# Where a 64-bit weight piece is finished, and how the queues around it are ordered, in a top-k attention kernel with an MLP behind it

## The chip, the cores and the metric

The kernel runs on one core of a Trainium2 chip. Its engines are TensorE (matrix multiply, PE in the profile; its weight loads are PEld), VectorE (DVE), ScalarE (ACT), GpSimd (POOL) and SyncE (SP), which issues the transfers. The metric is the device time of one execution in microseconds (us); less is better.

## The reference

Attention over 8 batches, 8 heads, 576 positions and a head width of 64, in which each query keeps only its 32 largest scores; the result, 4608 tokens of 512 numbers, goes through an MLP with 2048 hidden units and a SmeLU between its two matrix products. `moe_w_in` and `moe_w_out` come as 64-bit floats; q, k and v have 32 bits.

```python
scores = scale * np.matmul(q, k.transpose(0, 1, 3, 2))
kth = np.partition(scores, -top_k, axis=-1)[..., -top_k:-top_k + 1]
scores = np.where(scores >= kth, scores, -1000000000.0)
attn = np.exp(scores - np.max(scores, axis=-1, keepdims=True))
attn = attn / (np.sum(attn, axis=-1, keepdims=True) + 1e-09)
x = np.matmul(attn, v)                     # then (B,H,S,D) -> (B*S, H*D)
h = x @ w_in
g = np.where(h >= 1, h, np.where(h <= -1, 0.0, (h + 1) ** 2 / 4.0))
out = (g @ w_out).astype(np.float32)
```

## The kernel before

**Steps.** Attention is done in 144 steps, in the order of the list `steps`. A step takes 128 queries of two heads of a batch (or the 64 tail queries of four heads). `queries` and `keys_of` transpose q and k on TensorE; `scores` (L211) multiplies them in two halves of 288 columns and ScalarE copies the result into the tile `s` (three buffers). `weights` (L236) does the top-k on VectorE: `pairs` (L231) takes the larger of column c and column c + 288, four rounds of `max` (eight largest values, L248) and `match_replace` (L257) find the 32 largest of these pairs, and L262 to L269 repair the 32nd value `kth` with the smaller ones of the pairs. After the first round the row maxima are negated (`nmax`, L250, on POOL) and ScalarE takes the exponentials `e` (L252). L279 zeroes what lies below `kth` and sums up; L284 and L285 give the reciprocal `rz`, and POOL normalises `e` with it (L287). `transpose_w` (L291) turns the weights on TensorE, `values` (L305) multiplies them by v and ScalarE copies the result into `xT`.

**Can the pairs go wrong?** Where more large values sit in pairs than the repair looks at, `excess` (L270, on POOL) is positive. At the end `judge` reduces all of `excess` to a flag, and if it is set, `run` is done once more by a general path (`paired` false) without pairs. For the inputs used here the flag is not set.

**The MLP.** When all steps of a chunk (one or two tiles of 128 tokens) are done, `mlp` (L337) puts its work into `pending`: 16 units `hidden` (matmuls into `ph`, L344, then two relus on ScalarE, L348 and L350, and three POOL operations, L351 to L353; `r` has two buffers, `ph` three), then per tile eight units `final` (L361). A unit has a cost and the number of weight pieces that it needs.

**Weights.** The 64-bit weights are brought to 32 bits on the chip in 64 pieces of 128 x 256 (`weight_piece`, L80): a load of both words (`raw`, three buffers); VectorE shifts the high word (L87), ScalarE makes units of the low word (L90) and the absolute value (L94), POOL adds as integers (L91); one piece later VectorE puts the sign bit in (L96) and multiplies by "is at least 1.125 * 2^-15" (L98; the high word read as a 32-bit float, in which this bound stands for the smallest normal 32-bit number), which makes tiny weights zero.

**Order.** PE, DVE and ACT run in the order in which the program is written (`manual_schedule`, L425); POOL's and SP's order is left to the scheduler of the language. The loop of L466 writes it: iteration m does `values` of step m - 2, `scores` of step m + 1 and `weights` of step m, cut into seven slots; slot 2 has `transpose_w` of step m - 1, slot 4 transposes of later queries and keys, each slot but some first ones converts a piece, and `advance` (L413) takes units from `pending` by a share of what is left and by estimates of when each engine is where (`pe_time`, `dve_time`, `K_TIME`, `PIECE_TIME`).

## Time and profile before

| | |
|---|---|
| time, median of 3 runs | 1894.29 us (1892.67 to 1895.69) |
| profiled execution | 1893.17 us, its span 1891.4 us |
| mean granted TensorE clock | 0.947 of full speed |
| busy share of the span | PE 89%, PEld 62%, DVE 82%, ACT 53%, POOL 53% |
| moved by DMA | 57.81 MB |

The span runs from the first to the last instruction of the profiled execution; the time of an execution has a little around it. A busy share is a mean over stretches with different limits, so it tells little alone. A row of a timeline has the start, the duration, the engine, the line and operation, the tile written and those read, and in brackets how long the engine stood idle before it and what released it. A row of waits says who waited for whom, how long in total, how often, and the longest.

### The profile page before, as it was taken

The numbers are of one execution on the slowest core, as the hardware profiler recorded it, in microseconds if no ns is written. First come the engines' busy times: TensorE is split into PE (matmuls) and PEld (weight loads), VectorE is DVE, ScalarE is ACT, GpSimd is POOL, SyncE is SP. The second block draws the span as 40 slices with busy tenths as digits, with TensorE's granted clock in tenths as the row PEclk, the third lists the DMA queues.
The fourth block names the chain that finished last, engine by engine and source line by source line (L and its number), as shares of the span: only waits on it lengthen the run. The fifth ranks groups of instructions, "written<-read, shape, count | busy, mean of one in ns | idle before, by whom it ended". The sixth has DMA issues, their size and how long they took to land.

```text
span 1891.4 us, 33291 instructions
## 1 busy us (share of the span) xinstructions
PE 1688.7 (89%) x10513; PEld 1178.2 (62%) x10513; DVE 1558.9 (82%) x4947; ACT 1004.1 (53%) x2525; POOL 996.3 (53%) x1853
## 2 busy tenths in 40 slices
PE   3464599989999999999999999989999999998998
PEld 2252366666677666757576676656576666666665
DVE  5858777888878998999998898999887888869760
ACT  5454455556555654555464665555555555455443
POOL 3463355656556372817282674628283564653653
PEclk7576799999999999999999999999999999999999
DMA  7323100100001100110010100110010000000000
GB/s 188 99 68 92 62 18 18 38 21 24 10 17 39 29 12 23 32 36 13 17 34 25 24 12 25 36 32 12 23 32 18 18 12 10 12 12 6 1 12 14
DMA packets 107450, 57.81 MB, mean 31 GB/s; under 512 B 86272, under 2 KB 94464, under 8 KB 107264
## 3 DMA queue, kind: packets, MB, share of 16 engines
q1 hardware_dynamic: 107264, 55.59, 10.7%
q8 instruction: 85, 1.39, 0.3%
q14 instruction: 101, 0.83, 0.1%
HBM read 46.14 MB, written 9.44 MB: 29 GB/s over the span
## 4 chain that ended last, share of the span: by engine, by line
PE 60%; DVE 17%; POOL 12%; ACT 5%; issue 5%; DMA 1%; POOLq 0%; SPq 0%; DVEq 0%; ACTq 0%
PE py L361 24%; PE ph L344 15%; PE sp L223 8%; PE po L313 6%; PE pw L298 4%; DVE tops L248 4%; POOL g L353 4%; DVE more L257 4%; POOL r L352 3%; DVE e L279 3%; POOL r L351 2%; POOL e L287 2%; ACT e L252 1%; DVE seconds L265 1%; ACT s L226 1%
## 5 line engine op out<-in xcount | busy, mean ns | idle before, releaser
L344 PE MATMUL ph<-xT,w_in 128*128 128x128 f32 (+1 forms) x3200 | 564.6, 332 | 26.3 <-ACT g L350 23.9
L361 PE MATMUL py<-w_out,g 128*128 128x512 f32 x1152 | 538.4, 607 | 50.3 <-DVE w_out L98 47.6
L344 PEld LDWEIGHTS ph<-xT,w_in 128*128 128x128 f32 x3200 | 484.3, 197 | 100.4 <-ACT g L350 35.7
L248 DVE MAX8 tops<-more 128x8 f32<-128x288 f32 x1152 | 465.6, 446 | 0.0
L361 PEld LDWEIGHTS py<-w_out,g 128*128 128x128 f32 x1152 | 207.3, 192 | 280.8 <-issue 218.0
L257 DVE MATCH_REPLACE8 more<-tops,more 128x288 f32<-128x288 f32 x864 | 375.9, 443 | 0.0
L287 POOL TENSOR_SCALAR e<-e,rz 128x576 f32<-128x576 f32 x288 | 218.1, 767 | 237.8 <-DVE rz L285 215.5
L348 ACT ACTIVATE r<-ph,half 128x128 f32<-128x128 f32 (+1 forms) x400 | 166.9, 417 | 286.3 <-POOL g L353 210.2
L270 POOL TENSOR_TENSOR excess<-seconds,kth 128x2 f32<-128x2 f32 x144 | 60.7, 421 | 403.3 <-DVE kth L269 402.3
L279 DVE SCALAR_TENSOR_TENSOR e<-s,kth,e 128x576 f32<-128x576 f32 x288 | 242.4, 869 | 37.0 <-ACT e L252 36.9
L353 POOL TENSOR_TENSOR g<-r,g 128x128 f32<-128x128 f32 (+1 forms) x400 | 256.8, 642 | 28.5
L223 PE MATMUL sp<-kT,qT 64*128 64x288 f32 x1024 | 199.3, 454 | 53.3 <-ACT xT L326 43.7
L352 POOL TENSOR_TENSOR r<-r 128x128 f32<-128x128 f32 (+1 forms) x400 | 226.7, 567 | 29.9
L252 ACT ACTIVATE e<-s,nmax 128x576 f32<-128x576 f32 x288 | 215.8, 782 | 44.6 <-POOL nmax L250 44.6
L234 DVE TENSOR_TENSOR more<-s 128x576 f32<-128x576 f32 x144 | 115.9, 805 | 145.2 <-ACT s L226 145.1
L226 ACT ACTIVATE s<-sp 128x288 f32<-128x288 f32 x576 | 197.1, 418 | 49.0 <-PE sp L223 44.8
L351 POOL TENSOR_SCALAR r<-r 128x128 f32<-128x128 f32 (+1 forms) x400 | 177.4, 443 | 62.2 <-ACT r L348 61.6
L298 PEld LDWEIGHTS pw<-ident,e 128*128 128x128 f32 x1152 | 136.7, 145 | 76.3 <-issue 38.2
L299 ACT COPY wT<-pw 128x512 f32<-128x512 f32 x288 | 154.8, 595 | 52.1 <-PE pw L298 52.1
L298 PE MATMUL pw<-ident,e 128*128 128x128 f32 x1152 | 157.4, 281 | 26.4 <-POOL e L287 25.0
L313 PEld LDWEIGHTS po<-wT,v_in 128*64 128x64 f32 x2048 | 119.9, 142 | 95.7 <-issue 55.9
L313 PE MATMUL po<-wT,v_in 128*64 128x128 f32 x2048 | 156.8, 290 | 25.2 <-ACT wT L299 24.2
(60 smaller groups left out, 1476.9 us busy)
## 6 DMA issues: line engine op xcount, KB each, us to landing
q_in<-in_q_dram SPq DMA_DIRECT2D x32, 256.0 KB, 3.1
k_in<-in_k_dram SPq DMA_DIRECT2D x64, 128.0 KB, 3.1
raw<-in_moe_w_in_dram SPq DMA_DIRECT2D x32, 256.0 KB, 2.7
v_in<-in_v_dram SPq DMA_DIRECT2D x8, 1024.0 KB, 5.7
raw<-in_moe_w_out_dram SPq DMA_DIRECT2D x32, 256.0 KB, 2.6
out_dram<-y SPq DMA_DIRECT2D x32, 256.0 KB, 2.3
k_tl<-in_k_dram SPq DMA_DIRECT2D x8, 128.0 KB, 3.1
v_tail<-in_v_dram SPq DMA_DIRECT2D x16, 64.0 KB, 2.8
```

What stands on the lines that cost most here:

```text
L223: nc.tensor.matmul(o[:, a0 - c0:a1 - c0], qT[d, g, :], kT[d, g, k0:k0 + a1 - a0], start=True, stop=True)
L248: nc.vector.max(out=tops[:, i, r:r + 8], in_=src[:, i, :])
L252: nc.scalar.activation(e[:, i, :], s[:, i, :], AF.Exp, bias=nmax[:, i:i + 1])
L257: nc.vector.match_replace(out=rest[:, i, :], in_to_replace=tops[:, i, r:r + 8], in_values=src[:, i, :], imm_value=LOWEST)
L279: nc.vector.scalar_tensor_tensor(out=e[:, i, :], in0=s[:, i, :], scalar=last[:, i:i + 1], in1=e[:, i, :], op0=ALU.is_ge, op1=ALU.mult, acc ...
L287: nc.gpsimd.tensor_scalar(e[:, i, :], e[:, i, :], rz[:, i:i + 1], 1.0, ALU.mult, ALU.mult)
L298: nc.tensor.transpose(pt[:, c, :], w[:, i, main(i)][:, c * P:(c + 1) * P], ident)
L313: nc.tensor.matmul(po[j * D:(j + 1) * D], v_in[:, h, c, :] if c < NT else v_tl[0][:, h, :], wT[:, j, c, :] if c < NT else wTt, start=(c == ...
L344: nc.tensor.matmul(ph, w_in[:, kk, f * P:(f + 1) * P], xT[:, kk, 0:cw], start=(kk == 0), stop=(kk == NK - 1))
L352: nc.gpsimd.tensor_tensor(out=r, in0=r, in1=r, op=ALU.mult)
L353: nc.gpsimd.tensor_tensor(out=g[:, 0:cw], in0=r, in1=g[:, 0:cw], op=ALU.add)
L361: nc.tensor.matmul(py, gs[f][:, i * P:(i + 1) * P], w_out[:, f, :], start=(f == 0), stop=(f == NF - 1))
```

## The change

- A piece has one VectorE operation left, the shift. ScalarE takes the sign of the high word instead of its absolute value, and POOL multiplies magnitude and sign into the weight tile.
- Tiny weights are no longer zeroed on the way. After all pieces are converted, `inspect_piece` loads each piece once more, one per step, and ScalarE sums the signs of weight + 1.125 * 2^-15 and of weight - 1.125 * 2^-15; `judge` takes the difference of the sums into `excess`, so that a tiny weight sets the flag, and the general path (`any_size`) zeroes it. No weight of the inputs used here is that small.
- `nmax` and `excess` are made on VectorE instead of POOL.
- Iteration m begins the scores of step m + 2 instead of m + 1 and transposes the queries of step m + 3 instead of m + 2.
- POOL joins the order written by hand. After the conversion the top-k of a step is written into slots 0 to 3 (`parts`), which places its normalisation on POOL in slot 3 instead of slot 6. `advance` and the estimates of time are rewritten: a unit is taken only if its pieces are usable by the estimate, and the share is bounded by what is pending until the next chunk is ready.

```diff
@@ -71,51 +77,52 @@
             nc.gpsimd.memset(x, 0.0)
 
 
+
+    WC = 256
+    n_pieces = NK * DFF // WC + NF * DM // WC
     n_steps = B * (NT * NHP + NHP // 2)
-    excess = const.tile([P, 2 * n_steps], F32, name="excess")
-
-
-    WC = 256
-
-    def weight_piece(pool, dst, src):
+    excess = const.tile([P, 2 * n_steps + n_pieces], F32, name="excess")
+    signs = const.tile([P, 2, n_pieces], F32, name="signs")
+
+
+    pieces_of_weights = [(w_in[:, kk, c:c + WC], moe_w_in[kk * P:(kk + 1) * P, c:c + WC])
+                         for c in range(0, DFF, WC) for kk in range(NK)]
+    pieces_of_weights += [(w_out[:, f, c:c + WC], moe_w_out[f * P:(f + 1) * P, c:c + WC])
+                          for f in range(NF) for c in range(0, DM, WC)]
+
+    def load_words(pool, i):
         raw = pool.tile([P, 2 * WC], U32, name="raw", bufs=3)
-        nc.sync.dma_start(out=raw, in_=src.bitcast(U32))
+        nc.sync.dma_start(out=raw, in_=pieces_of_weights[i][1].bitcast(U32))
         words = raw.rearrange("p (n t) -> p n t", t=2)
-        lo, hi = words[:, :, 0], words[:, :, 1]
+        return words[:, :, 0], words[:, :, 1]
+
+    def convert_piece(pool, i, any_size):
+
+        lo, hi = load_words(pool, i)
+        dst = pieces_of_weights[i][0]
 
         bits = pool.tile([P, WC], U32, name="bits", bufs=2)
         nc.vector.tensor_scalar(bits, hi, 3, None, ALU.logical_shift_left)
 
         units = pool.tile([P, WC], F32, name="units", bufs=2)
         nc.scalar.activation(units, lo, AF.Identity, bias=two, scale=2.0 ** -51)
+        sign = pool.tile([P, WC], F32, name="sign", bufs=2)
+        nc.scalar.activation(sign, hi.bitcast(F32), AF.Sign)
         nc.gpsimd.tensor_tensor(out=bits.bitcast(I32), in0=bits.bitcast(I32), in1=units.bitcast(I32), op=ALU.add)
-
-        size = pool.tile([P, WC], F32, name="size", bufs=2)
-        nc.scalar.activation(size, hi.bitcast(F32), AF.Abs)
-        yield
-        nc.vector.scalar_tensor_tensor(out=bits, in0=hi, scalar=0x80000000, in1=bits,
-                                       op0=ALU.bitwise_and, op1=ALU.bitwise_or)
-        nc.vector.scalar_tensor_tensor(out=dst, in0=size, scalar=1.125 * 2.0 ** -15, in1=bits.bitcast(F32),
-                                       op0=ALU.is_ge, op1=ALU.mult)
-
-    def weight_pieces(pool):
-
-        pieces = [(w_in[:, kk, c:c + WC], moe_w_in[kk * P:(kk + 1) * P, c:c + WC])
-                  for c in range(0, DFF, WC) for kk in range(NK)]
-        pieces += [(w_out[:, f, c:c + WC], moe_w_out[f * P:(f + 1) * P, c:c + WC])
-                   for f in range(NF) for c in range(0, DM, WC)]
-        before = None
-        for dst, src in pieces:
-            piece = weight_piece(pool, dst, src)
-            if before is not None:
-                next(before, None)
-            next(piece)
-            before = piece
-            yield
-        next(before, None)
-        yield
-
-    n_pieces = NK * DFF // WC + NF * DM // WC
+        if any_size:
+            nc.scalar.activation(units, hi.bitcast(F32), AF.Abs)
+            nc.vector.scalar_tensor_tensor(out=sign, in0=units, scalar=TINY, in1=sign, op0=ALU.is_ge, op1=ALU.mult)
+
+            nc.vector.tensor_scalar(bits.bitcast(F32), bits.bitcast(F32), LARGEST, -LARGEST, ALU.min, ALU.max)
+        nc.gpsimd.tensor_tensor(out=dst, in0=sign, in1=bits.bitcast(F32), op=ALU.mult)
+
+    def inspect_piece(pool, i):
+
+        _, hi = load_words(pool, i)
+        for x in range(2):
+            sign = pool.tile([P, WC], F32, name="sign", bufs=2)
+            nc.scalar.activation(sign, hi.bitcast(F32), AF.Sign, bias=tiny[:, x:x + 1],
+                                 accum_out=signs[:, x, i:i + 1])
 
 
     def run(ctx, paired):
@@ -247,7 +254,7 @@
                 for i in range(2):
                     nc.vector.max(out=tops[:, i, r:r + 8], in_=src[:, i, :])
                 if r == 0:
-                    nc.gpsimd.tensor_scalar(nmax, tops[:, :, 0], -1.0, 1.0, ALU.mult, ALU.mult)
+                    nc.vector.tensor_scalar(nmax, tops[:, :, 0], -1.0, None, ALU.mult)
                     for i in range(2):
                         nc.scalar.activation(e[:, i, :], s[:, i, :], AF.Exp, bias=nmax[:, i:i + 1])
                         if i == 0:
@@ -267,7 +274,7 @@
                                         in1=seconds, op=ALU.min)
                 for i in range(2):
                     nc.vector.max(out=kth[:, i, :], in_=tops[:, i, TOP_K - 1:TOP_K + 8])
-                nc.gpsimd.tensor_tensor(out=excess[:, 2 * m:2 * m + 2], in0=seconds[:, :, 7], in1=kth[:, :, 0],
+                nc.vector.tensor_tensor(out=excess[:, 2 * m:2 * m + 2], in0=seconds[:, :, 7], in1=kth[:, :, 0],
                                         op=ALU.subtract)
                 last = kth[:, :, 0]
             else:
@@ -395,34 +402,43 @@
         ready = [max(m for m in range(n) if steps[m][3] == ch) for ch in range(len(chunks))]
 
         mlp_pool = ctx.enter_context(tc.tile_pool(name="mlp", bufs=1))
-        pieces_left = weight_pieces(mlp_pool) if paired else None
         pending = deque()
         total, spent = sum(len(tiles) for tiles in chunks) * (NK * NF + NF * DM // P), 0
-        converted, due = (-1 if paired else n_pieces), 0.0
+        converted, inspected, due = 0, 0, 0.0
 
         def convert():
             nonlocal converted
             if converted < n_pieces:
+                convert_piece(mlp_pool, converted, not paired)
                 converted += 1
-                next(pieces_left)
-
-
-        K_TIME, PIECE_TIME, UNIT_TIME, SLOTS = 9.6, 1.2, 0.22, 7
-        pe_time, dve_time, done, scored = 9.0, 12.0, {}, {}
+
+        def inspect():
+            nonlocal inspected
+            if paired and inspected < n_pieces:
+                inspect_piece(mlp_pool, inspected)
+                inspected += 1
+
+
+        K_TIME, PIECE_TIME, UNIT_TIME, SLOTS = 9.8, 0.4, 0.22, 7
+        pe_time, dve_time, done, scored, usable = 9.0, 12.0, {}, {}, {}
 
         def advance(amount, until=0.0):
 
             nonlocal spent, due, pe_time
             due += amount
-            while pending and pending[0][1] <= converted and (due >= pending[0][0] or pe_time < until):
-                cost, _, work = pending.popleft()
+            while pending and (due >= pending[0][0] or pe_time < until):
+                cost, pieces, work = pending[0]
+                if pieces > converted or usable[pieces] > pe_time + 0.5:
+                    break
+                pending.popleft()
                 due = max(due - cost, 0.0)
                 spent += cost
                 pe_time += cost * UNIT_TIME
                 work()
-            due = min(due, 8.0)
-
-        order = tc.manual_schedule(engines={mybir.EngineType.PE, mybir.EngineType.DVE, mybir.EngineType.Activation})
+            due = min(due, 16.0)
+
+        order = tc.manual_schedule(engines={mybir.EngineType.PE, mybir.EngineType.DVE, mybir.EngineType.Activation,
+                                            mybir.EngineType.Pool})
         order.__enter__()
         keys, xTs = {}, {}
         q_ins, qTs = {}, {}
@@ -452,51 +468,66 @@
             state.append(dict(m=m, t=t, hp=hp, keys=keys[b], qT=qTs[b, t], xT=(xTs[ch], col)))
             scores(state[m])
 
-        queries(0)
-        begin(0)
-        scored[0] = pe_time
+        def begin_at(m):
+            nonlocal pe_time
+            if m < n:
+                queries(m)
+                begin(m)
+                pe_time += 1.15
+                scored[m] = pe_time + 2.0
+
+        def convert_by(time):
+            convert()
+            usable[converted] = time
+
+        begin_at(0)
         if paired:
-            convert()
-            convert()
             pairs(state[0])
-        for _ in first:
-            pass
+        convert_by(13.0)
+        convert_by(14.0)
+        next(first)
+        begin_at(1)
         fetch(1)
         next_keys = 1
         for m in range(n + 2):
-            share = (total - spent) / (n + 2 - m)
+            coming = min((r + 2 - m for r in ready if r + 2 > m), default=1)
             if 2 <= m:
+                pe_time = max(pe_time, transposed + 1.8) + 1.25
                 values(state[m - 2])
                 state[m - 2] = None
-                pe_time += 1.25
                 for ch in [c for c in range(len(chunks)) if ready[c] == m - 2]:
                     pending.extend(mlp(xTs[ch], chunks[ch], mlp_pool))
-            if m + 1 < n:
-                begin(m + 1)
-                pe_time += 1.15
-                scored[m + 1] = pe_time + 2.0
-            top_k, quota = None, 0
+            share = min((total - spent) / (n + 2 - m), sum(work[0] for work in pending) / coming)
+            if m > 0:
+                begin_at(m + 2)
+            else:
+                for _ in first:
+                    pass
+                begin_at(2)
+            top_k, parts = None, [0] * SLOTS
             if m < n:
                 top_k = weights(state[m], state[m + 1] if m + 1 < n else None)
-                quota = min(SLOTS, n_pieces - converted)
+                left = min(SLOTS, n_pieces - converted)
+                parts = [1] * SLOTS if left > 0 else [1, 2, 2, 2, 0, 0, 0]
                 start = max(dve_time, scored[m])
-                dve_time = start + K_TIME + PIECE_TIME * quota
+                dve_time = start + K_TIME + PIECE_TIME * left
                 done[m] = dve_time
             for slot in range(SLOTS):
-                if top_k is not None:
+                now = start + (dve_time - start) * (slot + 1) / SLOTS
+                for _ in range(parts[slot]):
                     next(top_k, None)
-                    if slot > 0 or m % 2 == 0:
-                        convert()
-                    until = start + (dve_time - start) * slot / SLOTS
-                else:
-                    until = 0.0
+                if m < n and converted < n_pieces:
+                    convert_by(now)
+                elif slot == 6:
+                    inspect()
                 if slot == 2 and 1 <= m <= n:
                     pe_time = max(pe_time, done[m - 1] + 2.0) + 1.0
                     transpose_w(state[m - 1])
+                    transposed = pe_time
                 if slot == 2 and m == n and paired:
                     judge(ps, att)
                 if slot == 4:
-                    queries(m + 2)
+                    queries(m + 3)
                     if m < n and prep is None and next_keys < B and steps[m][0] == next_keys - 1 and steps[m][1] >= 1:
                         prep = keys_of(next_keys)
                     if prep is not None and m % 2 == 0:
@@ -506,7 +537,7 @@
                             prep, next_keys = None, next_keys + 1
                         else:
                             keys[next_keys] = got
-                advance(share / SLOTS, until)
+                advance(share / SLOTS if m < n else 0.0, now)
             for _ in (top_k if top_k is not None else ()):
                 pass
         while pending:
@@ -518,6 +549,7 @@
 
     def judge(ps, att):
         worst = att.tile([P, 8], F32, name="worst", bufs=1)
+        nc.vector.tensor_tensor(out=excess[:, 2 * n_steps:], in0=signs[:, 0], in1=signs[:, 1], op=ALU.subtract)
         nc.vector.max(out=worst, in_=excess)
         pt = ps.tile([1, P], F32, name="pworst", tag="a", bufs=4)
         nc.tensor.transpose(pt, worst[:, 0:1], ident)
```

## Rows read from the trace of the kernel before

**Rows 1.** Windows: stretch; busy us of PE, PEld, DVE, ACT, POOL; clock, DMA.

```profile
0.00:247.00 247.00, 131.73 (x670) 90.28 (x671) 175.93 (x555) 125.92 (x313) 111.30 (x196) 0.70 0.34 97
247.00:1843.00 1596.00, 1515.64 (x9614) 1060.43 (x9613) 1382.14 (x4391) 863.98 (x2171) 865.66 (x1607) 0.98 0.08 21
```

**Rows 2.** Windows of the tile rz on VectorE alone (one per step).

```profile
0.00:247.00 247.00, 1.66 (x10) 0.70 0.34 97
247.00:1843.00 1596.00, 22.18 (x134) 0.98 0.08 21
```

**Rows 3.** Waits, 0 to 247 us: total, times, longest.

```profile
PE py L361 <- DVE w_out L98: 47.6, 13, 6.4
DVE bits L96 <- POOL bits L91: 44.8, 32, 17.4
```

**Rows 4.** Waits, 247 to 1843 us.

```profile
POOL excess L270 <- DVE kth L269: 391.7, 77, 5.9
...
ACT r L348 <- POOL g L353: 188.4, 158, 3.3
DVE more L234 <- ACT s L226: 140.2, 80, 8.0
...
DVE e L279 <- ACT e L252: 36.6, 36, 3.1
```

**Rows 5.** Groups by line: busy us, mean ns, idle before and releaser.

```profile
L270 POOL TENSOR_TENSOR excess<-seconds,kth 128x2 f32<-128x2 f32 x144 | 60.7, 421 | 403.3 <-DVE kth L269 402.3 <-ACT wTt L302 1.1
...
L91 POOL TENSOR_TENSOR bits<-bits,units 128x256 int32<-128x256 int32 x64 | 50.2, 785 | 117.2 <-ACT units L90 48.3 <-DVE bits L87 39.8 <-DVE z L284 23.8
...
L284 DVE TENSOR_SCALAR z<-z 128x2 f32<-128x2 f32 x144 | 39.1, 271 | 4.7
...
L250 POOL TENSOR_SCALAR nmax<-tops 128x2 f32<-128x2 f32 x144 | 28.2, 196 | 0.4 <-DVE tops L248 0.4
...
L96 DVE SCALAR_TENSOR_TENSOR bits<-raw,bits 128x256 uint32<-128x256 uint32 x64 | 26.9, 421 | 44.8 <-POOL bits L91 44.8
...
L98 DVE SCALAR_TENSOR_TENSOR w_out<-size,bits 128x256 f32<-128x256 f32 x32 | 14.9, 467 | 3.4
...
L185 ACT ACT_TABLE_LOAD x1 | 1.3, 1283 | 0.7 <-PEq L547 0.7
```

**Rows 6.** Timeline of the conversion, VectorE and POOL: start us, us.

```profile
15.23 0.82 DVE L248 MAX8 tops<-more 128x8 f32<-128x288 f32 x2
...
74.04 2.02 POOL L287 TENSOR_SCALAR e<-e,rz 128x576 f32<-128x576 f32 x2
...
77.88 0.29 DVE L87 TENSOR_SCALAR bits<-raw 128x256 uint32<-128x256 uint32 x1
78.08 0.81 DVE L248 MAX8 tops<-more 128x8 f32<-128x288 f32 x2
...
78.88 0.73 POOL L91 TENSOR_TENSOR bits<-bits,units 128x256 int32<-128x256 int32 x1 [1.97 <-ACT units L90]
...
115.09 0.29 POOL L351 TENSOR_SCALAR r<-r 128x128 f32<-128x128 f32 x1 [1.15 <-ACT r L348]
...
116.38 0.29 POOL L351 TENSOR_SCALAR r<-r 128x128 f32<-128x128 f32 x1
```

**Rows 7.** Timeline of two steady steps on VectorE: start us, us.

```profile
643.02 0.17 DVE L285 RECIPROCAL rz<-z 128x2 f32<-128x2 f32 x1
...
648.66 0.76 DVE L262 TENSOR_TENSOR more<-s 128x576 f32<-128x576 f32 x1
...
653.20 0.17 DVE L285 RECIPROCAL rz<-z 128x2 f32<-128x2 f32 x1
...
658.84 1.20 DVE L262 TENSOR_TENSOR more<-s 128x576 f32<-128x576 f32 x1
```

**Rows 8.** Windows of line 344 on TensorE alone.

```profile
0.00:247.00 247.00, 31.07 (x224) 0.70 0.34 97
```

**Rows 9.** DMA issues by line: count, KB each, us to landing.

```profile
raw<-in_moe_w_in_dram SPq DMA_DIRECT2D x32, 256.0 KB, 2.7
```

## What the change should do to the time: the prediction

> **What bounds the kernel now.** I read the page's slices first, then busy time by stretches, then the times at which the steps end, then the waits of those stretches, last the timeline of single steps. A step ends on VectorE with the reciprocal `rz` (L285), one per step, 144 in all. The view of that line by windows splits the run [rows 2]: the first 247 us hold 10 of them, the next 1596 us the other 134, of which the first falls right at its border: the work of 11 steps lies before 247 us and that of 133 behind it. 48.4 us of the span remain for what follows the last step (the last tile's MLP). So a step costs 22.5 us in the first stretch and 12.0 us in the second.
>
> In the first stretch [rows 1] the reader is to see that no engine is full: TensorE is busy 132 of 247 us at a granted clock of 0.70 (a mix of its two levels, 1.2 and 2.4 GHz), VectorE 176. VectorE waits 44.8 us for the integer add on POOL in the middle of a piece, and TensorE 47.6 us for converted `w_out` [rows 3]. This stretch is a chain through the weight pieces. In the second stretch TensorE is busy 1516 of 1596 us and VectorE 1382, so two engines are nearly full; VectorE waits 140.2 us for scores and 36.6 us for exponentials [rows 1, 4], and 37 us are short gaps. TensorE has 80 us of idle time in all of it: that caps what any cure of VectorE's waits can bring.
>
> **Conversion, part by part.** Per piece the change takes the and/or (421 ns) and the compare-multiply (about 460 ns) off VectorE and leaves the shift, which holds the queue 0.20 us from start to start (77.88 to 78.08) [rows 5, 6]. Sign on ScalarE takes the place of Abs, one for one; I price it the same. POOL keeps the add and gets a multiply of the same shape and two sources, which before has no row; the add is the nearest, 0.73 us alone, 785 ns mean [rows 5, 6]. It cannot cost less than nothing; above, I bound it by that mean.
>
> A step with seven pieces then is: on VectorE 10.18 us (an undisturbed step, 643.02 to 653.20 [rows 7]) + 7 x 0.20 + 0.40 (negation and difference, below) = 12.0. On POOL: 7 x 2 x 0.73 + 2.0 (normalisation, the 74.04 row [rows 6]) = 12.2. Both now end together, and they disturb each other: the pairwise maximum L262 took 0.76 us with POOL idle and 1.20 us with POOL at work [rows 7]. Four VectorE operations of a step have two long sources (L262, L234, twice L279), so 4 x 0.44 = 1.8 is added: 14.0 us. The bits, units and sign tiles have two buffers, so VectorE's shift also waits for the multiply two pieces back; POOL's in-order queue puts the normalisation between two pieces, and that 2 us is already in POOL's sum. The raw loads land in 2.7 us [rows 9]; with about 1 us of ScalarE behind them and three buffers, that is some 1.2 us a piece, below POOL's 1.46.
>
> Two pieces precede step 0, then seven a step: 62 / 7, so nine steps convert, against 9.8 in the old pattern of six and seven. The first maximum started at 15.2 us behind two pieces [rows 6]; now the pairs come first, say 14. Nine steps at 14.0 reach 140. In the last four of them the first tile's 16 hidden units want POOL at 1.29 us each (115.09 to 116.38 [rows 6]), 20.6 us, which either fit into gaps (0) or lie wholly on POOL's chain: 140 to 161, I take 150. Two steps without pieces at 11.5 follow: the eleventh step ends at 173 (163 to 184) instead of 247. **This is 74 us, the surest part.** TensorE will by then have done a little less MLP than the 28 hidden units (224 records of 8) seen before 247 [rows 8], about 5 us of debt, absorbed below.
>
> *A rule against it:* here the row shows POOL at 0.73 to 0.79 us for what VectorE's multiply did in about 0.46. The Trainium skill, "GPSIMD Engine Reference", section Engine selection, says that elementwise work on a tile belongs on VectorE, POOL being about twice slower with two inputs; the trace agrees on the ratio (1.7). By the rule the multiply stays on VectorE, whose step would be 12.0 + 7 x 0.5 = 15.5 us plus contention, nine steps 14 us or more slower than the sum above: the rule is right on the operation and wrong on the queue.
>
> **The steady stretch.** Maxima are negated on VectorE and `excess` is formed there: two operations of 128x2, 133 times. The nearest rows are operations of 128x2 there: 0.17 us for the reciprocal of an undisturbed step [rows 7], 271 ns mean for L284 [rows 5]; between them I take 0.20, the distance at which a short operation lets the next one start [rows 6]. So 0.40 us a step = 53 us (45 to 72), all on an engine that is nearly full. What it buys: POOL loses 89 us (28.2 + 60.7) and, more, the place where its queue stood 391.7 us for the 33rd value [rows 4, 5] with MLP units behind it; ScalarE, which stood 188.4 us for POOL's last operation of a unit, is released earlier. Scores two steps ahead give the pairs one more step of slack, 12 us, where the longest wait was 8.0: I take three quarters of the 140.2 (105) as gone, the rest standing where TensorE itself is a step behind; and half of the 36.6 (18), since the exponentials no longer pass POOL but still stand behind ScalarE's other work. VectorE's account: 1596 - 105 - 18 + 53 = 1526. TensorE's floor is its 1516 plus the debt. Two bounds so near each other alternate by phase of the MLP, so a quarter of TensorE's 80 idle us stays on top: 1546.
>
> Later inspection: 64 pieces are loaded again, one a step, with two Signs each. At about 430 ns like Abs plus a read of the sum that no row shows (VectorE's own is 80 ns), about 1 us of ScalarE a step. ScalarE is busy 864 of 1596 [rows 1], which hides it; uncovered it would be 64 us. Its loads join SP's queue behind query loads; 16 MB over 700 us, with the DMA share at 0.08, collide with nothing. The slot pattern (two parts of the top-k per slot) moves no work on VectorE's own queue.
>
> **Sum.** 173 + 1546 + 48.4 = 1767 span, plus 1.8 around it (the profiled execution took 1893.17 for a span of 1891.4) = 1769; that execution lies 1.1 below the median of 1894.29. Forecast: **1770**.
>
> **The rivals.**
> - *Only the start gains.* TensorE had 80 us idle in 1596, and VectorE gets 53 us more work: the second stretch may stay at 1596. 163..184 + 1596 + 48 + 2 gives 1809 to 1830. For it: TensorE 95% busy. Against: 177 us of waits. 0.27.
> - *Both waits vanish.* The stretch falls to TensorE's 1516: 163 + 1516 + 50 = 1729, a little lower if busy TensorE hides stretched matmuls. 0.09.
> - *Slower: POOL in program order.* POOL joins the manual schedule, and a step's normalisation is now placed with the fourth slot, ahead of the MLP units of slots 3 to 6, though it waits for that step's `rz`. Those units, and through two `r` buffers ScalarE's relus, stand until VectorE ends the step; the second exponential of the next step stands behind them. VectorE wants it 8 us into its 10.2 us step. After `rz` POOL needs 2 us, then 1.29 a unit or more: (8 - 2 - 0.8) / 1.29 = 4 units fit. 400 hidden units lie in about half of the steps, 5.6 a step, of which 5/7 stand ahead, 4.0; the two `r` buffers take two off. From four units on each further one costs 1.29 us in some 67 steps; 1.4 of them beyond eat all 124 us of the forecast, and two give 1770 + 173 = 1943. Against it: POOL stood as long before, for `excess`. 0.09.
> - *Sign is not in the loaded table.* The trace shows one table load, 1283 ns [rows 5], so all functions used so far sit together; none is Sign. If it sits elsewhere, at most four switches a step with two exponentials in nine steps and two in 64 later ones: 164 x 1.28 = 210 us on ScalarE, between hidden and all on the path; half of it gives 1875, all of it 1980. 0.03. The Trainium skill, "ScalarE: Activation LUTs", section Table sets, lists relu, copy, identity and abs as in every set and does not name Sign there; with the 2.66 us per switch that the page gives for load and drain it would be 436 us.
>
> The forecast's own case has 0.52 (1740 to 1805). What a measurement of this kernel can tell from no change is about 0.2%. The slow sign holds 0.09 and part of the table case, 0.11; within 0.2% 0.02; faster 0.87. The range must reach over the start-only case and to the PE floor: 1715 to 1840, leaving out the slow cases and the extremes.
>
> **What would show it.** Right: the eleventh `rz` near 173; VectorE's waits for POOL's add gone, short waits for the multiply in their place; POOL about 85% busy until 150; waits for scores under 50 us in all; undisturbed steps of 10.6 us. Wrong: the ninth step later than 180 (POOL's queue costs more than its operations); steps of 12 us or more after it, with VectorE waiting for `e` (POOL's order) or TensorE without gaps (start only); more than one table load.

## The result, and the profile after

The changed kernel takes 1831.41 us (median of 4; 1829.49 to 1835.5), the kernel before beside it 1893.48: ratio 0.967 [0.966, 0.969]. That is 62 us less, where 124 were forecast; 1831 lies within the range 1715 to 1840, near its slow end. The profiled execution took 1835.5 us, its span 1833.5. Of all executions below one stands out and is left out of its ratio: one of the four of *h1* took 9250 us instead of 1823, and no trace shows why.

Windows of the changed kernel, cut where the eleventh and the last step end (columns as in [rows 1]):

```profile
0.00:205.30 205.30, 127.75 (x674) 89.85 (x675) 150.95 (x450) 130.31 (x324) 146.41 (x238) 0.75 0.44 125
205.30:1776.70 1571.40, 1507.47 (x9600) 1056.10 (x9599) 1428.88 (x4655) 926.09 (x2418) 788.46 (x1339) 0.98 0.11 31
1776.70:1833.50 56.80, 48.20 (x242) 29.97 (x240) 1.21 (x5) 13.58 (x42) 21.41 (x56) 0.97 0.03 12
```

The start got 42 us shorter (247 to 205; 173 forecast), the second stretch 25 (1596 to 1571; 1546 forecast), the tail got 8 longer (48.4 to 56.8). All three terms came out dearer than forecast: by 32, 25 and 8 us.

Waits of VectorE in the changed kernel, whole run:

```profile
DVE e L286 <- ACT e L259: 46.2, 39, 5.9
DVE bits L105 <- POOL w_out L117: 24.0, 8, 10.5
DVE e L286 <- issue: 22.2, 12, 3.4
DVE e L286 <- POOL g L360: 21.3, 8, 4.6
DVE e L286 <- POOL r L359: 16.2, 8, 4.3
DVE more L241 <- ACT s L233: 12.4, 1, 12.4
```

The reader is to see two things beside [rows 3, 4]. The wait for scores (140.2) is gone from the second stretch; the 12.4 is the first step. But L286, the operation that needs the exponentials, now waits 106 us there (109 in the whole run), under several names, where it waited 36.6. VectorE's account of that stretch is 1429 busy + 106 + 36 short gaps = 1571, against 1382 + 177 + 37 before: of 140 us that left, 70 came back one line further down, and 47 more of work are, in the main, the moved operations.

ScalarE and POOL in the changed kernel, whole run:

```profile
POOL e L294 <- DVE rz L292: 524.6, 80, 15.1
...
ACT r L355 <- POOL g L360: 149.7, 137, 6.4
```

In the kernel before, whole run:

```profile
POOL e L287 <- DVE rz L285: 215.5, 68, 7.9
...
ACT r L348 <- POOL g L353: 210.2, 190, 3.3
```

ScalarE still waits for POOL's last operation of a unit. POOL no longer stands for `excess` (402.3 us before [rows 5]), but stands longer for `rz`.

Groups by line of the changed kernel (busy us, mean ns, idle before and releaser):

```profile
L257 DVE TENSOR_SCALAR nmax<-tops 128x2 f32<-128x2 f32 x144 | 39.5, 275 | 4.9
...
L105 DVE TENSOR_SCALAR bits<-raw 128x256 uint32<-128x256 uint32 x64 | 32.5, 509 | 36.8 <-POOL w_out L117 24.0 <-DMA raw<-in_moe_w_in_dram 6.4 <-POOL w_in L117 5.8
...
L277 DVE TENSOR_TENSOR excess<-seconds,kth 128x2 f32<-128x2 f32 x144 | 30.1, 209 | 5.0
...
L117 POOL TENSOR_TENSOR w_in<-sign,bits 128x256 f32<-128x256 f32 x32 | 25.6, 801 | 2.5
...
L192 ACT ACT_TABLE_LOAD x1 | 1.3, 1283 | 0.7 <-PEq L579 0.7
```

POOL's multiply costs what the add was priced at. The shift, the same operation as before, has a mean of 509 ns. A conversion step of the changed kernel, parts of its timeline, shows why:

```profile
50.05 0.28 DVE L105 TENSOR_SCALAR bits<-raw 128x256 uint32<-128x256 uint32 x1
...
55.00 0.73 POOL L111 TENSOR_TENSOR bits<-bits,units 128x256 int32<-128x256 int32 x1
55.08 0.80 DVE L105 TENSOR_SCALAR bits<-raw 128x256 uint32<-128x256 uint32 x1 [1.29 <-POOL w_in L117]
55.80 0.81 DVE L255 MAX8 tops<-more 128x8 f32<-128x288 f32 x2
...
57.30 0.73 POOL L117 TENSOR_TENSOR w_in<-sign,bits 128x256 f32<-128x256 f32 x1
57.38 0.80 DVE L105 TENSOR_SCALAR bits<-raw 128x256 uint32<-128x256 uint32 x1
...
60.95 0.75 DVE L269 TENSOR_TENSOR more<-s 128x576 f32<-128x576 f32 x1
60.95 1.32 POOL L117 TENSOR_TENSOR w_in<-sign,bits 128x256 f32<-128x256 f32 x1
```

With POOL idle, as at 50.05, the shift takes 0.28; where it begins just behind an add or multiply of POOL it takes 0.80 and ends 0.15 us after that operation. At 60.95 it is POOL's operation that is stretched. They take turns; the 8-largest operations show nothing of it. The Trainium skill, "SBUF — State Buffer", section SBUF: two separate sides, states such a rule: VectorE and GpSimd share a pair of ports as an exclusive lock held for a whole instruction, wanted by VectorE's operations with two inputs or in a fast mode. The trace agrees on the turns, 0.80 us against 0.28; whether the shift, which has one source, works in such a mode no run shows.

In the same kernel, where the MLP begins, VectorE and POOL:

```profile
103.92 0.73 POOL L117 TENSOR_TENSOR w_out<-sign,bits 128x256 f32<-128x256 f32 x1
104.62 0.30 POOL L358 TENSOR_SCALAR r<-r 128x128 f32<-128x128 f32 x1
...
115.84 0.46 POOL L360 TENSOR_TENSOR g<-r,g 128x128 f32<-128x128 f32 x1
116.25 0.72 POOL L111 TENSOR_TENSOR bits<-bits,units 128x256 int32<-128x256 int32 x1
117.05 0.73 POOL L117 TENSOR_TENSOR w_out<-sign,bits 128x256 f32<-128x256 f32 x1
117.82 0.37 DVE L105 TENSOR_SCALAR bits<-raw 128x256 uint32<-128x256 uint32 x1 [10.48 <-POOL w_out L117]
```

Nine hidden units (1.28 us each) run between two pieces, and VectorE's shift waits 10.5 us for a buffer. And a step of the second stretch:

```profile
408.79 0.32 DVE L257 TENSOR_SCALAR nmax<-tops 128x2 f32<-128x2 f32 x1
...
413.67 0.37 ACT L355 ACTIVATE r<-ph,half 128x128 f32<-128x128 f32 x1 [2.11 <-POOL g L360]
...
415.45 0.37 ACT L355 ACTIVATE r<-ph,half 128x128 f32<-128x128 f32 x1 [1.16 <-POOL g L360]
...
419.69 0.77 ACT L259 ACTIVATE e<-s,nmax 128x576 f32<-128x576 f32 x1
420.55 0.82 DVE L286 SCALAR_TENSOR_TENSOR e<-s,kth,e 128x576 f32<-128x576 f32 x1 [3.70 <-POOL g L360]
```

The maxima are there at 409.1, the exponential starts at 419.7: ScalarE works in program order, and between the two it stands in relus that wait for one of two `r` buffers, which POOL empties. Four such waits make up 4.1 of the 10.6 us; the rest is, in the main, work that stands ahead of the exponential.

### The profile page after: what moved, and what is told of

Read it like the earlier page. It is cut to its first block, busy times and chain, and to the rows that moved or that the text cites. A ratio compares the mean times of both kernels' runs of the same rounds, so it can differ in the third digit from the quotient of the medians.

```text
span 1833.5 us, 33329 instructions
## 1 busy us (share of the span) xinstructions
PE 1683.4 (92%) x10513; PEld 1175.9 (64%) x10513; DVE 1581.0 (86%) x5108; ACT 1070.0 (58%) x2781; POOL 956.3 (52%) x1631
## 4 chain that ended last, share of the span: by engine, by line
PE 56%; DVE 26%; POOL 9%; ACT 4%; issue 3%; DMA 1%; POOLq 0%; SPq 0%; ACTq 0%; DVEq 0%
PE py L368 21%; PE ph L351 16%; PE sp L230 7%; DVE tops L255 7%; DVE more L264 6%; PE po L320 5%; PE pw L305 4%; DVE e L286 4%; POOL g L360 3%; POOL r L359 2%; DVE seconds L272 2%; DVE more L269 2%; DVE more L241 2%; POOL e L294 2%; POOL r L358 1%
## 5 line engine op out<-in xcount | busy, mean ns | idle before, releaser
L368 PE MATMUL py<-w_out,g 128*128 128x512 f32 x1152 | 544.5, 611 | 8.2 <-POOL w_out L117 5.7
L294 POOL TENSOR_SCALAR e<-e,rz 128x576 f32<-128x576 f32 x288 | 212.1, 747 | 565.3 <-DVE rz L292 524.6
L286 DVE SCALAR_TENSOR_TENSOR e<-s,kth,e 128x576 f32<-128x576 f32 x288 | 247.7, 889 | 108.7 <-ACT e L259 46.2
L355 ACT ACTIVATE r<-ph,half 128x128 f32<-128x128 f32 (+1 forms) x400 | 166.9, 417 | 251.3 <-POOL g L360 149.7
L230 PE MATMUL sp<-kT,qT 64*128 64x288 f32 x1024 | 204.9, 454 | 67.4 <-ACT xT L333 54.5
L358 POOL TENSOR_SCALAR r<-r 128x128 f32<-128x128 f32 (+1 forms) x400 | 166.7, 417 | 182.2 <-ACT r L355 181.7
L305 PEld LDWEIGHTS pw<-ident,e 128*128 128x128 f32 x1152 | 142.3, 149 | 90.1 <-POOL e L294 53.4
L305 PE MATMUL pw<-ident,e 128*128 128x128 f32 x1152 | 164.6, 288 | 38.1 <-POOL e L294 36.6
L230 PEld LDWEIGHTS sp<-kT,qT 64*128 64x128 f32 x1024 | 112.4, 194 | 117.3 <-ACT xT L333 68.9
L357 ACT ACTIVATE g<-ph,minus 128x128 f32<-128x128 f32 (+1 forms) x400 | 164.6, 411 | 0.0
L320 PEld LDWEIGHTS po<-wT,v_in 128*64 128x64 f32 x2048 | 114.0, 140 | 75.6 <-issue 50.4
L320 PE MATMUL po<-wT,v_in 128*64 128x128 f32 x2048 | 146.5, 285 | 7.0 <-ACT wT L306 6.9
```

What stands on the lines that cost most here:

```text
L230: nc.tensor.matmul(o[:, a0 - c0:a1 - c0], qT[d, g, :], kT[d, g, k0:k0 + a1 - a0], start=True, stop=True)
L286: nc.vector.scalar_tensor_tensor(out=e[:, i, :], in0=s[:, i, :], scalar=last[:, i:i + 1], in1=e[:, i, :], op0=ALU.is_ge, op1=ALU.mult, acc ...
L294: nc.gpsimd.tensor_scalar(e[:, i, :], e[:, i, :], rz[:, i:i + 1], 1.0, ALU.mult, ALU.mult)
L305: nc.tensor.transpose(pt[:, c, :], w[:, i, main(i)][:, c * P:(c + 1) * P], ident)
L320: nc.tensor.matmul(po[j * D:(j + 1) * D], v_in[:, h, c, :] if c < NT else v_tl[0][:, h, :], wT[:, j, c, :] if c < NT else wTt, start=(c == ...
L368: nc.tensor.matmul(py, gs[f][:, i * P:(i + 1) * P], w_out[:, f, :], start=(f == 0), stop=(f == NF - 1))
```

## The experiments

All were timed in three rounds beside the kernel before (1893 to 1897 us); an edit is to the changed kernel unless said. Each half-width of a ratio is 0.0015 to 0.003, some 3 to 6 us.

**Conversion.** *a1*: a third buffer for what a piece passes on.

```diff
-bits = ... bufs=2; units = ... bufs=2; sign = ... bufs=2
+bits = ... bufs=3; units = ... bufs=3; sign = ... bufs=3
```

> Theory (queues): in the changed kernel a conversion step takes 15.8 us, of which 1.3 us is VectorE's shift waiting for the multiply two pieces back, and in steps 5 and 6 POOL's MLP units stand between pieces; those waits sum to 30 us. A third buffer for bits, units and sign lets VectorE run one piece (about 2 us) further ahead: conversion steps near 14.8 us, the ninth step ends near 168 instead of 180.5 us, time 1818 to 1824. Rival (the short one-source shift pays for POOL's operation itself, whatever the buffers): steps stay at 15.5 or more, time 1828 or more.

1826.46 us, 0.963 [0.962, 0.965]; a conversion step 15.3 instead of 15.8, the ninth step's end at 175, between theory and rival. The waits for buffers cost about 5 us; the stretched shifts stay (mean 482 ns).

*a2*: no MLP unit before the last piece.

```diff
-                if pieces > converted or usable[pieces] > pe_time + 0.5:
+                if converted < n_pieces or usable[pieces] > pe_time + 0.5:
```

> No MLP unit is taken before the last piece is written. Theory (POOL's order holds the pieces up behind the 16 hidden units): steps 5 and 6 fall from 29.6 and 20.6 us to 15.8, the ninth step ends near 162 instead of 180.5. The first tile's MLP, 28 us of TensorE, is then owed later, where TensorE had 64 us idle: time 1815 to 1840. Rival (TensorE is the bound of all that follows): the ninth step ends early too, but the 28 us come on top: 1840 to 1860.

1830.32 us, 0.966 [0.964, 0.967]. The ninth `rz`, in the changed kernel and in *a2*:

```profile
180.45 0.17 DVE L292 RECIPROCAL rz<-z 128x2 f32<-128x2 f32 x1
```

```profile
163.05 0.17 DVE L292 RECIPROCAL rz<-z 128x2 f32<-128x2 f32 x1
```

The hole is the units. The time is unchanged: the units are owed later, and the second stretch is 8 us longer (1579).

*e4*: the shift as an operation with two sources.

```diff
-nc.vector.tensor_scalar(bits, hi, 3, None, ALU.logical_shift_left)
+nc.vector.scalar_tensor_tensor(out=bits, in0=hi, scalar=3, in1=none,   # none: zeros
+                               op0=ALU.logical_shift_left, op1=ALU.bitwise_or)
```

> The shift of a piece written as an operation with two sources (shift, then or with zeros); nothing else. Theory: short VectorE operations with one source wait for the running POOL operation and those with two sources do not, so the shift takes 0.40 to 0.46 us whether POOL works or not, mean under 460 ns instead of 509, none near 0.8 us; the conversion step stays at 15.5 to 16.0 us because the mean hardly changes, the time at 1826 to 1834 us. Rival: the shift is slow beside POOL because of its tiles (strided reads, traffic), and then two sources are slower still: mean above 560 ns, single ones at 0.8 us and more, and the time 1830 to 1840 us.

1836.58 us, 0.971 [0.969, 0.972]; mean of the shift 629 ns, single ones up to 0.96. My theory, that only operations with one source wait, falls; the rival's numbers hold, its reason was not tested by itself. Its timeline shows the turns in both directions, on a maximum L272 with two sources:

```profile
62.07 0.79 POOL L120 TENSOR_TENSOR w_in<-sign,bits 128x256 f32<-128x256 f32 x1
62.20 1.28 DVE L272 TENSOR_TENSOR more<-s 128x576 f32<-128x576 f32 x1
62.83 1.23 POOL L114 TENSOR_TENSOR bits<-bits,units 128x256 int32<-128x256 int32 x1
```

*c4*: without the second loads and their 128 signs (the search for tiny weights is left out).

```diff
-                elif slot == 6:
-                    inspect()
```

> The changed kernel without the later inspection: the 64 second loads and their 128 Signs are left out. These take 731 ns each on ScalarE with the read of the sum, 92 us, all in the hidden and final units of 64 steps. Theory (ScalarE's queue is the lag before the exponentials): time 1800 to 1820. Rival (hidden, as forecast): 1827 to 1835.

1826.27 us, 0.963 [0.962, 0.965]: the inspection costs about 5 us, though its Signs and their reads keep ScalarE busy for 92.

**The r buffers.** *b1*: POOL's order left to the scheduler.

```diff
-order = tc.manual_schedule(engines={PE, DVE, Activation, Pool})
+order = tc.manual_schedule(engines={PE, DVE, Activation})
```

> POOL is left out of the order written by hand, all else as changed. Theory (POOL in program order keeps ScalarE's relus, and with them the exponentials, waiting): VectorE's waits for e fall from 103 to at most 40 us, time 1770 to 1800. Rival (TensorE, 1507 of 1571 us busy in the second stretch, is the bound): waits change place, time 1822 to 1840. Second rival (the hand-written order is better than the scheduler's): slower, 1845 or more, with holes in the conversion.

1825.7 us, 0.964 [0.962, 0.966]. The theory falls: L286 still waits 102 us. *b2*, *d1*: six `r` buffers, in the changed kernel and in the one before.

```diff
-r = pool.tile([P, CW], F32, name="r", bufs=2)[:, 0:cw]
+r = pool.tile([P, CW], F32, name="r", bufs=6)[:, 0:cw]
```

> Six buffers instead of two for the relu tile r. Theory (ScalarE waits for POOL through the two r buffers, the exponentials stand behind): ScalarE's wait for POOL's g falls from 125 us to under 30, VectorE's waits for e from 103 to under 50, time 1775 to 1800. Rival (TensorE is the bound, or the exponentials are late for the units themselves that stand ahead of them on ScalarE): ScalarE's wait goes, VectorE's stays at 80 or more, time 1820 to 1835.

> The kernel before with six buffers for r, nothing of the change. Theory (the two r buffers held ScalarE in both kernels, and the change only moved the wait from the scores to the exponentials): ScalarE's 188 us for POOL's g and VectorE's 140 us for scores fall below a third, the second stretch goes from 1596 to about 1500, time 1790 to 1815. Rival (the scores two steps ahead, or POOL's order by hand, are what makes the buffers pay): gain of at most 30 us, 1860 or more.

*b2*: 1750.29 us, 0.924 [0.922, 0.925]. *d1*: 1807.76 us, 0.954 [0.952, 0.955], more than the whole change gave, with one number. Waits of VectorE and ScalarE and the second stretch (to its last step) in *b2*:

```profile
DVE e L286 <- ACT e L259: 23.6, 23, 5.9
...
DVE e L286 <- POOL g L360: 1.7, 2, 1.4
```

```profile
ACT r L355 <- POOL g L360: 7.6, 15, 1.1
```

```profile
202.40:1692.20 1489.80, 1460.31 (x9596) 1023.45 (x9595) 1426.65 (x4654) 925.56 (x2415) 804.33 (x1333) 1.00 0.11 32
```

ScalarE's wait falls from 149.7 to 7.6 us, the wait for exponentials from 109 to 27, and the stretch is 26 us shorter than TensorE's 1516, which I had taken as a floor. TensorE's own busy time fell with it, from 1507 to 1460, at a granted clock of 1.00 instead of 0.98; by an estimate some 30 of these 47 us are the clock (1507 x 0.98 = 1477). *e2*, *f2*: three and four buffers; *e3*: four, with three for `bits` and `units`.

> The changed kernel with three r buffers instead of two. Theory: a relu waits for the unit two back by 1.16 us on the mean (125 us in 108 waits), which is less than one unit of POOL (1.3 to 1.7 us), so one more buffer takes most of it: ScalarE's wait for POOL under 40 us, VectorE's waits for exponentials under 50 us, time 1755 to 1785 us. Rival: the units queue on POOL in runs of four or five behind one reciprocal, and each buffer buys a quarter of the 81 us that four more bought: 1805 to 1820 us.

> The changed kernel with four r buffers. Theory: the gain grows with each buffer (two 1831, three 1786, six 1750 us), four alone give 1757 to 1766 us, and the deeper buffers of a piece added nothing beside them (1762 us with both). Rival: four buffers do as much as six, 1747 to 1753 us, and the deeper buffers of a piece cost the 11 us.

> The changed kernel with four r buffers and three buffers for bits and units (what fits beside each other). Theory: four r buffers do what six did, and the buffers of a piece give their 5 us on top, since the start and the steady stretch are separate sums: 1743 to 1752 us. Rival: what the start gives is taken back later because the MLP is owed, as when no MLP unit ran before the last piece: 1750 to 1758 us.

1786.32, 1768.2 and 1761.72 us: 0.943 [0.942, 0.945], 0.934 [0.932, 0.936], 0.930 [0.929, 0.932]. Two, three, four, six buffers: 1831, 1786, 1768, 1750. The third gives half; the buffers of a piece add their 6 us beside four.

*f1*: six `r` buffers and the edit of *a2*.

> The changed kernel with six r buffers and no MLP unit before the last weight piece is converted. Without the buffers the held units made the conversion 17 us shorter and the whole no shorter. Theory: they were owed to a stretch in which ScalarE stood for POOL; with six r buffers VectorE alone sets the steady pace, TensorE, ScalarE and POOL have room for 16 units more, and 8 to 17 us stay: 1733 to 1743 us against 1750. Rival: the owed units cost as much later whatever the buffers, since TensorE is as full as VectorE: 1746 to 1755 us.

1748.35 us, 0.923 [0.922, 0.925]: the units are owed at the same price, TensorE being busy 1475 of 1499 us between the eleventh and the last step. My theory, that room would be there, falls.

**Scores.** *c1*: scores one step ahead again; *e1*: the same with six `r` buffers.

```diff
-begin_at(m + 2); queries(m + 3)
+begin_at(m + 1); queries(m + 2)
```

> The changed kernel with scores one step ahead, as before (queries two ahead). Theory (the waits for scores and for exponentials are one lag of ScalarE, seen at two places): waits for scores return to 80 to 140 us, those for e fall somewhat as both end together, time 1850 to 1890. Rival (the second step was worth nothing, the gain of the second stretch came from elsewhere): 1826 to 1840.

> The changed kernel with six r buffers and scores one step ahead again. Theory: with two r buffers the second step of slack was eaten by ScalarE's queue, so it bought nothing; with six it pays. Taking it back brings VectorE's wait for scores back, 74 us in the kernel before with six r buffers and 76 us in the changed kernel with scores one ahead, of which the wait of ScalarE for a free score tile (73 us with six r buffers, off the path mostly) does not give back more than half: 1785 to 1825 us against 1750. Rival: two ahead only moves the wait between VectorE and ScalarE whatever the r buffers: 1745 to 1765 us.

*c1*: 1820.85 us, 0.960 [0.956, 0.963], about 10 us less than the change itself; *e1*: 1749.39 us, 0.924 [0.923, 0.926], as *b2* and as its rival has it. Neither theory nor rival held for *c1*. Waits of VectorE in *c1*:

```profile
DVE more L241 <- ACT s L233: 75.6, 36, 12.3
...
DVE e L286 <- ACT e L259: 20.8, 20, 2.7
```

What waits for scores in one order waits for exponentials in the other. Two steps ahead gain nothing here; why they cost 10 us with two `r` buffers is open.

**The small operations and POOL's order.** *c3*: `nmax` and `excess` back on POOL; *f3*: that with six `r` buffers; *g1*: with six, and POOL's order free; *h1*: with two, and the order free; *g2*: six and free, small operations on VectorE.

```diff
-nc.vector.tensor_scalar(nmax, tops[:, :, 0], -1.0, None, ALU.mult)
+nc.gpsimd.tensor_scalar(nmax, tops[:, :, 0], -1.0, 1.0, ALU.mult, ALU.mult)
-nc.vector.tensor_tensor(out=excess[...], ...)
+nc.gpsimd.tensor_tensor(out=excess[...], ...)
```

> The changed kernel with the negated maxima and excess on POOL again, in POOL's hand-written order. VectorE loses 64 us of work in the steady stretch (275 and 209 ns means). Theory (VectorE stands for e anyway, and POOL's queue then waits for the 33rd value in program order): slower, 1840 to 1900. Rival (VectorE's added operations eat the gain): faster, 1770 to 1800.

> The changed kernel with six r buffers and with maxima and excess back on POOL. With two buffers this cost 31 us. Theory: POOL's in-order queue is what makes the maxima late, so they cost as much with six: the start 8 us longer, the steady stretch some 1515 us as in the kernel before with six r buffers, 1775 to 1800 us. Rival: POOL's lateness came from the same jam as ScalarE's; with it gone VectorE, now the bound, gets 45 to 53 us of work back and the time falls to 1705 to 1745 us.

> Six r buffers, maxima and excess on POOL, and POOL's order left to the scheduler as in the kernel before. With POOL in program order this took 1805 us, ScalarE waiting 242 us for the negated maxima in the steady stretch, where the kernel before with six r buffers had 51. Theory: POOL's program order is what makes the maxima late; without it ScalarE's wait falls under 100 us and the time to 1755 to 1785 us (the 32 us that the start is shorter than in the kernel before with six r buffers come through). Rival: the order matters as little as it did with two buffers and maxima on VectorE (5 us); the wait stays above 180 us and the time at 1795 to 1810 us.

> Six r buffers and POOL's order left to the scheduler, maxima and excess on VectorE. Theory: nothing on VectorE's path passes POOL any more, so its order is free: 1746 to 1754 us, as with the program order (1750). Rival: the units' order still counts through the tail and the last value of a step: more than 6 us to either side.

> Two r buffers as in the change; maxima and excess on POOL and POOL's order left to the scheduler, as in the kernel before. So pieces, scores two ahead and the new shares of MLP stay. Theory: program order on POOL and the small operations on POOL are bad only together, as with six r buffers; without the order 1810 to 1830 us, no worse than with the small operations on VectorE and free order (1826), so that the 31 us of moving them were the repair of a loss that the order makes. Rival: with two r buffers the maxima are late whatever the order, because MLP units jam POOL: 1845 to 1865 us.

| us | small ops on VectorE | on POOL |
|---|---|---|
| two `r`, program order | 1831 (the change) | 1863 (*c3*, 0.982 [0.980, 0.984]) |
| two `r`, free order | 1826 (*b1*) | 1823 (*h1*, 0.962 [0.960, 0.964]) |
| six `r`, program order | 1750 (*b2*) | 1805 (*f3*, 0.953 [0.952, 0.955]) |
| six `r`, free order | 1745 (*g2*, 0.922 [0.921, 0.924]) | **1739** (*g1*, 0.919 [0.917, 0.920]) |

After *c3* the move of the small operations seemed worth 31 us. The table says otherwise: with POOL's order free it is worth nothing or a few us the wrong way. It only repairs what the program order does to them, 40 us with two buffers and 66 with six (1863 against 1823, 1805 against 1739). POOL and ScalarE in *f3*:

```profile
810.87 0.74 POOL L294 TENSOR_SCALAR e<-e,rz 128x576 f32<-128x576 f32 x1
811.58 0.40 POOL L358 TENSOR_SCALAR r<-r 128x256 f32<-128x256 f32 x1
...
816.88 0.72 POOL L360 TENSOR_TENSOR g<-r,g 128x256 f32<-128x256 f32 x1
817.57 0.19 POOL L257 TENSOR_SCALAR nmax<-tops 128x2 f32<-128x2 f32 x1
817.80 1.44 ACT L259 ACTIVATE e<-s,nmax 128x576 f32<-128x576 f32 x2 [6.26 <-POOL nmax L257]
```

Three MLP units stand behind the normalisation and ahead of a 0.19 us negation, and ScalarE stands 6.3 us for it. In the whole run, *f3* and then *g1*, where the scheduler sets the order:

```profile
ACT e L259 <- POOL nmax L257: 277.8, 83, 6.9
```

```profile
ACT e L259 <- POOL nmax L257: 74.4, 52, 4.3
```

The fastest version, *g1*, keeps the new pieces and takes the small operations and the order back; its second stretch:

```profile
204.80:1682.90 1478.10, 1461.72 (x9588) 1026.16 (x9587) 1375.78 (x4388) 923.63 (x2417) 894.02 (x1596) 1.00 0.12 33
```

VectorE is busy 51 us less than in *b2*, and the stretch is 12 us shorter.

## Why the prediction was right in direction and wrong in size

- **Direction: right.** The wait for the add in the middle of a piece is gone, the wait for scores too, Sign caused no further table load, the inspection is hidden but for 5 us, undisturbed steps take 10.5 to 10.6 us (661.87 to 672.40), as forecast.
- **"14.0 us" a conversion step: mis-sized, 15.8.** I found the contention and added it to the wrong operations: 0.44 on four long ones. In the step from 50.44 to 66.24 the seven shifts hold the queue for 3.14 (1.4 forecast), the two small operations 0.94 (0.40), L273 0.24 more, and a buffer wait 1.29: with 10.18 that is 15.8. The four long ones, on which I had put 1.8, are not stretched there. Over eight steps that is 14 us. With the first step (it ended at 34.2 instead of about 28), the units of the next point (9) and 2 us in the two steps behind them, this makes 31 of the start's 32.
- **Hidden units "either fit into gaps (0) or lie wholly on POOL's chain", half taken: they lie on it.** The two steps with units took 18.6 us more than plain ones, against 10 forecast; without the units (*a2*) the ninth step ends 17.4 us earlier. But holding them back wins nothing either, so the ninth step's date was no measure of the whole.
- **"What it buys" of the small operations: nothing by itself.** I credited their move with POOL's freed queue and ScalarE's earlier release, and charged 53 us of VectorE time (47 measured). POOL's queue stands at the normalisation instead, and *h1*, *g1* and *g2* show that with free order the move buys nothing. The rival "POOL in program order" had the right cause and the wrong victim: I let the units behind the normalisation hold ScalarE's relus, but in the changed kernel a free order is worth 5 us (*b1*). What those units hold is the negation of the maxima (*f3*), which the change had taken off POOL. Order and move together cost 8 us with two buffers (1831 against 1823) and 11 with six.
- **"Half of the 36.6" gone: the step that failed most; the wait grew to 106.** VectorE's account of the second stretch: scores gave back 140 (105 forecast), the moved operations took 47 (53), and the exponentials, which were to give back 18, took 69, an error of 87 us. The wait of 188 us for POOL [rows 4], from which I expected an earlier release, is a matter of the two `r` buffers: they couple ScalarE's queue to POOL's. With scores no longer late, this was late next, and the slack of two steps ahead did not help (*c1*, *e1*). Shown by *b2*, 81 us, and by *d1* in the kernel before.
- **"TensorE's floor is its 1516": no floor.** *b2* needs 1490 for the stretch, 106 us less than before, where I took TensorE's 80 idle us for the most that could be won. The rest of 20 that I set on top rested on nothing measured.
- **The tail, 48.4 taken over, was 56.8.** After the last step TensorE has 18 more matmuls of the units `final` left, 7.9 us, in the kernel before and in the changed one:

```profile
L361 PE MATMUL py<-w_out,g 128*128 128x512 f32 x46 | 20.2, 592 | 0.0
```

```profile
L368 PE MATMUL py<-w_out,g 128*128 128x512 f32 x64 | 28.1, 594 | 0.0
```

The rewritten loop gives `advance` no share behind the last step (`share / SLOTS if m < n else 0.0`); that this leaves them over was not tested.

- **Open** is what of the second stretch's gain comes from the new shares of MLP work: *h1*, which leaves only pieces, shares, scores and inspection of the change, has 1556 us there between its eleventh and its last step, 40 less than before, and I did not split that.

## What to carry to other kernels

A wait that leaves a line goes to the next thing that is late: before crediting it, look who stands in order on the other queues, and for which buffer (here ScalarE, 188 us, two buffers, the largest gain of all for one number). An edit that looks worth 31 us beside another edit of the same change may only repair it; undo the two singly and together. An engine's busy time in a stretch that others pace, at a lower granted clock, is no floor for it.

## What the runs showed of the hardware

- VectorE's shift beside POOL: 0.28 us alone, 0.80 when it starts just behind an add or multiply of POOL (0.73); as an operation with two sources 0.42 alone and up to 0.96 (*e4*). POOL's add and multiply are held the same way (0.73 to 1.32).
- A Sign with a sum over 128x256 takes 531 ns on ScalarE, and the read of the sum 200 ns more, against 430 for the Sign alone.
- TensorE's busy time for nearly the same matmuls (9600 and 9596 records) was 1507 us in the second stretch of the changed kernel at a granted clock of 0.98, and 1460 in that of *b2* at 1.00.
